# Attention, token mix, feed-forward and DFT kernel: VectorE in source order in the first group, fewer weight steps there, an earlier second batch, other homes for temporaries

## The chip, the cores and the metric

The kernel runs on one core of a Trainium2 chip. The metric is the device time of one execution in microseconds (us); three executions of the kernel before took 1892.73 to 1894.17 us, with a median of 1893.1 us.

## The reference

The computation, cut to what matters (8 batches, 8 heads, 576 tokens, head size 64, model size 512, feed-forward size 2048, all float32):

```
# attention with keys and values averaged over 8 tokens: 72 keys a head
k_p = k.reshape(B, H, 72, 8, D).mean(axis=3); v_p = the same of v
attn = softmax(q @ k_p.T / 8);  x = (attn @ v_p), heads side by side: B x 576 x 512
# token mix of rank 32, feed-forward 1
u = x + (x.T @ U @ V).T
x = u + relu(u @ moe_w1) @ moe_w2
# DFT mix over tokens and model size, layernorm, feed-forward 2
u = x + real(fft(fft(x, axis=tokens), axis=model))
un = (u - mean(u)) / sqrt(var(u) + 1e-6)
out = u + relu(un @ moe2_w1) @ moe2_w2
```

The four feed-forward weights arrive as float64. Each is turned into two float32 halves whose sum carries it; so is each activation (`hh` and `hl`, or `hw` for both in one tile), and one product becomes three matmuls.

## The kernel before, in words

Tokens go through the feed-forwards in blocks of 256. A first loop takes the first twelve blocks through feed-forward 1 (in groups: blocks 0 and 1 together, then one block each); later loops take the remaining six and all of feed-forward 2 in pieces of 512 tokens. The feed-forward size is cut into 16 tiles, f = 0 to 15. **Prologue.** `prep(0)` loads the pooled keys' and values' raw data of batch 0 (`kT`, `vr`) and reduces them over 8 tokens on VectorE (`kp`, `vp`); `first` runs the five attention tiles of batch 0 (scores on TensorE, maximum on VectorE, exponentials on ScalarE, the exponentials transposed and copied to `e` or a scratch tile `scr`, a product with `v`, and a division `x`, here a `scr` too). `mix_split` ends with `hst` (a copy on ScalarE, the remainder on VectorE), `mix_mm` multiplies it by `vst` and adds the result to the five x tiles, and `block_prep` transposes blocks 0 and 1 into `utx`, split in halves. **Groups.** Group 0 is "wide", with two blocks: 16 tiles f of `st1` (`h<-utx,w`), relu into `hh` and `hl` (or `hw` for odd f), and `st2` (`o<-w,hh` and so on) one tile behind.

Around `st1` and `st2` the loop steps lanes, which are Python generators: a (attention of later batches), mix, w (weights), prep (`prep` of the next batch: `kT` and `vr` through two buffers named `raw`, then the `kp` and `vp` reductions), p (`block_prep` of the next group) and d (the DFT). Of the w lane, `w_first` runs in the prologue and in group 0. For each f it loads two raw tiles (`wraw`, 512 KB each), makes a high half by bit operations (three ScalarE passes L144, L147, L108 and two VectorE passes L151, L152 for each tile of 128 x 512 words) and has GpSimd subtract (`w<-scr,w`), then the finished halves are written out (`wc`). `w_combine` follows (`wo`).

The order of instructions on an engine is chosen by a scheduler that simulates the program and moves instructions ahead of one another where it sees room; in a region under `tc.manual_schedule` the named engines keep source order. Before, ScalarE is named from group 1 on, and VectorE nowhere. All loads and stores go through SP's queue in SP's order, and a load into a reused buffer waits on SP until the buffer is free, with everything behind it.

Of the kernel before, what the change touches and what calls it, by code (L numbers as in the profile page):

```python
# [10 lines left out]
I32 = mybir.dt.int32  # L11
# [28 lines left out]
NOP = 12  # L40
NRING = 4
QAHEAD = 3
F64_BIAS = float.fromhex("0x1p-112")
# [3 lines left out]
def kernel(  # L47
# [30 lines left out]
    W = {}  # L78
    state = {"n": 0, "free": False, "m": "s1", "u": 0, "slot": 0, "x1": 0, "u2": 0, "op": 0, "clock": 0, "busy": False, "late": None, "tick": 0, "banks": ("s0", "s1", "hu")}

# [78 lines left out]
    def w_first(tmp):  # L159
        raws, ts = {}, {}  # L160

        def loads(upto):
            while len(raws) < min(NF, upto) and (len(raws) < (NF - 1 if state["free"] else 5) or NF - 2 in ts):
                f = len(raws)
                raws[f] = [wp.tile([128, 1024], I32, tag=f"w{k}_{f}", name="wraw") for k in range(2)]
                for k in range(2):
                    nc.sync.dma_start(out=raws[f][k], in_=(w1a, w2a)[k][f].bitcast(I32))
        def done(f):
            for k in range(2):
                w = wp.tile([128, 2, 512], F32R, tag=f"w{k}_{f}", name="w")  # L170
                W[k, f] = w
                split(w[:, 0], w[:, 1], ts[f][k].bitcast(F32), nc.gpsimd)
        loads(2)
        yield
        for f in range(NF + 1):
            loads(f + 3)
            while len(raws) < min(NF, f + 1):
                yield
                loads(f + 3)
            if f == NF - 1:  # L180
                done(f - 1)
            if f < NF:
                if f < NF - 2:
                    t = scratch(f % 2)
                    t = [t[:, 512 * k:512 * k + 512].bitcast(I32) for k in range(2)]
                else:
                    t = [tmp().bitcast(I32) for k in range(2)]
                ts[f] = t
                for k in range(2):
                    high(raws[f][k], 512, t[k], True)  # L190
            yield
            if f and f != NF - 1:
                done(f - 1)
            if f < NF:
                for k in range(2):
                    bits(raws[f][k], 512, t[k])
                yield
# [132 lines left out]
    class Attn:  # L330
        def __init__(self, c):
# [5 lines left out]
            self.ust = p1.tile([128, 5, 4, RANK], F32R, name="ust")  # L337
            self.usf = scratch(21)[:, 0:20 * RANK].rearrange("p (t g r) -> p t g r", t=5, g=4)
            self.vst = p1.tile([128, 640], F32R, name="vst")
# [5 lines left out]
            self.done = {}  # L345
            self.xq = [scratch(12 + t) for t in range(5)]
            self.x0 = [z[:, 0:512] for z in self.xq]
# [39 lines left out]
        def prep(self, b):  # L387
# [3 lines left out]
            self.kp[b] = (kp, vp)  # L391

            def load(i):
                t = scratch(2 + i) if b == 0 else self.tmp()
                if i < 4:
# [65 lines left out]
        def tile_steps(self, b, t, alt=0, before=None):  # L461
# [8 lines left out]
            for p in range(NPAIR):  # L470
                o = sc[p // 2][:n, (p % 2) * 144:(p % 2) * 144 + 144]
                mm(o, q[:, p, :n], self.k[:, p], p % 2 == 0, True)
            if 5 * b + t + QAHEAD >= 5:
                self.q_load(5 * b + t + QAHEAD)
            if before:
                before()
            sf = scratch(3 + alt) if alt else self.s
            if alt:
# [15 lines left out]
            nc.tensor.transpose(e1[:, :n], sf[:n, 512:640], ident[:n, :n])  # L494
            e = scratch(4 + 2 * alt, 640) if alt else p1.tile([128, 640], F32, tag="e", name="e")
            e = e.rearrange("p (c k) -> p c k", c=5)
# [519 lines left out]

    def rest(j):
        for t in range(NT):
            res[j, t] = mp.tile([128, DM], F32, tag="u", name="ur")
            r0 = j * T + t * 128  # L1020
            nc.sync.dma_start(out=res[j, t], in_=ud[r0:r0 + 128, :])
# [64 lines left out]
    def lane_prep(at):  # L1086
        for b in range(1, B):
            while b - 1 not in started or (b == 2 and state["slot"] < 11):
                yield
# [39 lines left out]
    for _ in g:  # L1129
        pass  # L1130
    lanes["w"] = w_first(at.cv)
    lanes["uv"] = at.setup_uv()
# [3 lines left out]
    for _ in f:  # L1136
        step("uv")
        step("w")
    with urgent():
        at.mix_split(0)  # L1140
    step("w")
    lanes["prep"] = lane_prep(at)
    for t in range(5):
        with urgent():
            at.mix_mm(0, t, at.x0[t])
        if t % 2:
            step("w")
        step("prep")
    state["u"] = S
    lanes["a"] = lane_a(at)  # L1150
    lanes["mix"] = lane_mix(at)
    for j in range(2):
        g = block_prep(j, at.x0[2 * j:])
        more = True
        while more:
            with urgent():
                more = not next(g, 1)
            if more:
                step("w")
    state["free"] = True  # L1160
    hq = []
    df = []
# [25 lines left out]
    slot = 0  # L1188
    order = ExitStack()
    for gi, js in enumerate(groups):  # L1190
        if gi == 1:
            order.enter_context(tc.manual_schedule(engines={mybir.EngineType.Activation}))
        wide = len(js) > 1
        last = js[-1] == 2 * SB - 1
        tags = (("o0", "o1"), ("h1", "m"))
        for f in range(NF):
# [30 lines left out]
            for i in range(2 if wide else 1):  # L1227
# [229 lines left out]
```

## Time and profile before

| what | value |
|---|---|
| median of three executions | 1893.1 us (1892.73 to 1894.17) |
| the profiled execution | 1888.01 us, its span 1886.2 us |
| TensorE busy | 1821.1 us (97%), weight loads 1634.8 us |
| VectorE busy | 1039.7 us (55%) |
| ScalarE busy | 715.7 us (38%) |
| GpSimd busy | 194.8 us (10%) |
| DMA | 394.41 MB, 209 GB/s in the mean |

The span is from the first to the last instruction of the profiled execution. PE is TensorE, PEld its weight loads, DVE is VectorE, ACT is ScalarE, POOL is GpSimd, SP the engine that issues the DMAs. A bracket behind a row of a timeline is the engine's idle time ahead of it and what ended it.

### The profile page before, as it was taken

The page shows a single profiled execution, that of the slowest core. Times are in us where ns is not written, and L with a number is a line of the kernel's source. Part 1 is how long each engine was busy: PE and PEld are TensorE (multiplying, and loading weights), DVE is VectorE, ACT ScalarE, POOL GpSimd, SP SyncE. Part 2 cuts the span into 40 slices and gives each one's busy share as a digit, 9 for nine tenths or more (in the row PEclk, how much of TensorE's full clock was granted, in tenths as well). Part 3 has the DMA queues.
Part 4 walks back from the last instruction along what each step waited for, and adds up shares of the span by engine and source line. Part 5 has one row for each costly group of instructions (what it writes and reads, how often), then busy time and mean ns, then how long its engine had stood idle before and what let it go on. Part 6 is the DMA issues. An engine that isn't in the chain of part 4 may idle for free.

```text
span 1886.2 us, 31833 instructions
## 1 busy us (share of the span) xinstructions
PE 1821.1 (97%) x11492; PEld 1634.8 (87%) x11492; DVE 1039.7 (55%) x2379; ACT 715.7 (38%) x2186; POOL 194.8 (10%) x341
## 2 busy tenths in 40 slices
PE   5789999999999999999999999999999999999999
PEld 3678888888989898899998889899999899989998
DVE  7774575656565544554456655555565444444332
ACT  7672444444434332433324332333333323232321
POOL 3440131222210000000010100000100000000000
PEclk9899999999999999999999999999999999999999
DMA  9754475758575524667677766666676674756563
GB/s 361 255 174 128 144 229 158 244 179 248 164 243 163 176 73 150 220 219 245 216 237 253 276 223 229 227 222 230 225 241 216 213 238 172 238 179 231 182 208 132
DMA packets 265789, 394.41 MB, mean 209 GB/s; under 512 B 61664, under 2 KB 92480, under 8 KB 265632
## 3 DMA queue, kind: packets, MB, share of 16 engines
q1 hardware_dynamic: 264704, 388.97, 62.3%
q0 software_dynamic: 928, 3.40, 0.5%
q8 instruction: 91, 1.49, 0.3%
q14 instruction: 66, 0.54, 0.1%
HBM read 312.73 MB, written 79.56 MB: 208 GB/s over the span
## 4 chain that ended last, share of the span: by engine, by line
PE 62%; DVE 2%; DMA 2%; issue 0%; ACT 0%; SPq 0%; DVEq 0%; ACTq 0%
PE h L112 27%; PE o L112 16%; PE m L112 7%; PE hu L112 7%; PE s L112 4%; PE s L889 1%; DMA w<-wd 0%; DMA R<-x1d 0%; DMA wr<-wc 0%; DMA out<-ur 0%; DMA ur<-u2d 0%; DMA wd<-cv 0%; DVE hl L1278 0%; DVE bs L865 0%; DVE ur L105 0%
## 5 line engine op out<-in xcount | busy, mean ns | idle before, releaser
L112 PEld LDWEIGHTS h<-x,wr 128*128 128x128 f32 x4032 | 527.6, 191 | 24.5 <-DVE side L105 0.8
L112 PE MATMUL h<-x,wr 128*128 128x256 f32 x4032 | 547.9, 284 | 0.2 <-DVE side L105 0.2
L112 PE MATMUL o<-w,hh 128*128 128x512 f32 x1440 | 417.4, 400 | 4.9 <-ACT hh L998 2.5
L112 PE MATMUL h<-utx,w 128*128 128x256 f32 (+1 forms) x2232 | 321.7, 289 | 9.2 <-DVE hl L999 3.8
L112 PEld LDWEIGHTS h<-utx,w 128*128 128x128 f32 x2232 | 301.2, 191 | 29.5 <-DVE hl L999 6.4
L112 PEld LDWEIGHTS o<-w,hh 128*128 128x128 f32 x1440 | 251.0, 190 | 43.5 <-ACT hh L998 5.6
L112 PE MATMUL o<-w,hl 128*128 128x512 f32 x720 | 239.1, 395 | 1.7 <-DVE hl L999 1.7
L105 DVE TENSOR_TENSOR side<-h,side 128x256 f32<-128x256 f32 x192 | 106.3, 554 | 137.8 <-PE h L112 136.9
L112 PEld LDWEIGHTS o<-w,hl 128*128 128x128 f32 x720 | 131.5, 189 | 25.4 <-DVE hl L999 2.1
L1272 ACT ACTIVATE hh<-side 128x256 fp32r<-128x256 f32 x192 | 100.0, 521 | 118.8 <-DVE side L105 112.5
L1272 ACT ACTIVATE hh<-h 128x256 fp32r<-128x256 f32 x96 | 36.8, 383 | 253.2 <-PE h L112 250.8
L1278 DVE SCALAR_TENSOR_TENSOR hl<-h,hh 128x256 fp32r<-128x256 f32 x96 | 40.7, 424 | 158.8 <-ACT hh L1272 158.8
L1278 DVE SCALAR_TENSOR_TENSOR hl<-side,hh 128x256 fp32r<-128x256 f32 x192 | 105.9, 551 | 28.2 <-ACT hh L1272 28.1
L489 ACT ACTIVATE s<-s,mx 128x72 f32<-128x72 f32 x296 | 90.6, 334 | 58.5 <-DVE mx L486 57.5
L112 PE MATMUL m<-w,hh 128*128 128x512 f32 x400 | 109.8, 395 | 0.0
L112 PE MATMUL hu<-w,hh 128*128 128x512 f32 x384 | 104.8, 394 | 0.0
L102 POOL TENSOR_TENSOR wo<-wo 128x256 fp32r<-128x256 f32 x88 | 69.1, 801 | 289.6 <-ACT wo L108 242.8
L998 ACT ACTIVATE hh<-h 128x256 fp32r<-128x256 f32 x158 | 61.4, 389 | 80.5 <-PE h L112 77.8
L999 DVE SCALAR_TENSOR_TENSOR hl<-h,hh 128x256 fp32r<-128x256 f32 x158 | 65.7, 417 | 32.7 <-ACT hh L998 32.1
L102 DVE TENSOR_TENSOR x<-ul,x 128x256 fp32r<-128x256 f32 x154 | 59.3, 421 | 42.2 <-ACT x L108 42.0
L112 PEld LDWEIGHTS m<-w,hh 128*128 128x128 f32 x400 | 69.1, 190 | 9.2
L1317 ACT ACTIVATE side<-h 128x256 f32<-128x256 f32 x96 | 36.7, 383 | 99.4 <-PE h L112 99.4
(252 smaller groups left out, 2390.3 us busy)
## 6 DMA issues: line engine op xcount, KB each, us to landing
wr<-wc SPq DMA_DIRECT2D x336, 512.0 KB
wc<-wo SPq DMA_DIRECT2D x88, 256.0 KB
x<-x SPq DMA_DIRECT2D x56, 256.0 KB
ur<-ud SPq DMA_DIRECT2D x36, 256.0 KB
x1d<-ur SPq DMA_DIRECT2D x36, 256.0 KB
ul<-u2d SPq DMA_DIRECT2D x36, 256.0 KB
ur<-u2d SPq DMA_DIRECT2D x36, 256.0 KB
out<-ur SPq DMA_DIRECT2D x36, 256.0 KB
```

The source lines that it names most:

```text
L102: eng.tensor_tensor(out=o, in0=a, in1=b, op=ALU.subtract)
L105: eng.tensor_tensor(out=o, in0=a, in1=b, op=ALU.add)
L112: nc.tensor.matmul(o, a, b, start=start, stop=stop, skip_group_check=True)
L489: nc.scalar.activation(out=s[:n, a], in_=v[:, k], func=ACTF.Exp, bias=mx[:n, a:a + 1], accum_out=sm[:n, a:a + 1])
L889: nc.tensor.transpose(o[:, k * 128:k * 128 + 128], u[:, k * 128:k * 128 + 128], ident)
L998: nc.scalar.activation(out=hh, in_=p, func=ACTF.Relu)
L999: nc.vector.scalar_tensor_tensor(out=hl, in0=p, scalar=0.0, in1=hh.bitcast(F32), op0=ALU.max, op1=ALU.subtract)
L1272: nc.scalar.activation(out=hh[:, i], in_=c, func=ACTF.Relu)
L1278: nc.vector.scalar_tensor_tensor(out=hl[:, i], in0=c, scalar=0.0, in1=hh[:, i].bitcast(F32), op0=ALU.max, op1=ALU.subtract)
L1317: nc.scalar.activation(out=sb, in_=v, func=ACTF.Copy)
```

## The change

- VectorE keeps source order in group 0 (beside ScalarE, which did so only from group 1 on). From group 1 on nothing changes in this.
- In group 0 the w lane is stepped once for each block of a tile f, where it was stepped twice for three tiles in four.
- `w_first` may have 12 tiles f of raw weights loaded in the late prologue and 15 after it (before: 5, then 15); for the first five f one of two high passes is on VectorE (`L147 TENSOR_SCALAR`) instead of ScalarE; half of its temporaries are `wo` tiles instead of scratch.
- The three q tiles of batch 1 are loaded after `mix_split`, where they were loaded in the first attention tiles.
- The prep lane is stepped twice with each tile of `mix_mm`, and batch 2 may begin at slot 9 instead of 11.
- The rows to which block 1's result is added (`ur<-ud`) are loaded at f = 12 into `cv` tiles, where they were loaded after block 0's end.

```
+    "most": 5 (in state)
-  while len(raws) < min(NF, upto) and (len(raws) < (NF - 1 if state["free"] else 5) or NF - 2 in ts):
+  while len(raws) < min(NF, upto) and (len(raws) < state["most"] or NSCR + 1 in ts):
...
+        def temps(f):
+            if f < NSCR and f % 4 < 2:
+                t = scratch(f % 2)
+                return [t[:, 512 * k:512 * k + 512].bitcast(I32) for k in range(2)]
+            return [tmp().bitcast(I32).rearrange("p h x -> p (h x)") for k in range(2)]
...
-                    high(raws[f][k], 512, t[k], True)
+                    high(raws[f][k], 512, ts[f][k], k or f >= 5)
...
-            if 5 * b + t + QAHEAD >= 5:
+            if b:
                 self.q_load(5 * b + t + QAHEAD)
...
-            while b - 1 not in started or (b == 2 and state["slot"] < 11):
+            while b - 1 not in started or (b == 2 and state["slot"] < 9):
...
-    lanes["w"] = w_first(at.cv)
+    lanes["w"] = w_first(at.wo)
...
+    state["most"] = NF - 4
     with urgent():
         at.mix_split(0)
     step("w")
+    for i in range(QAHEAD):
+        at.q_load(5 + i)
...
         step("prep")
+        step("prep")
...
+        if gi == 0:
+            order.enter_context(tc.manual_schedule(engines={mybir.EngineType.Activation}))
+            first_group.enter_context(tc.manual_schedule(engines={mybir.EngineType.DVE}))
         if gi == 1:
-            order.enter_context(tc.manual_schedule(engines={mybir.EngineType.Activation}))
+            first_group.close()
...
+            if wide and f == 12:
+                rest(js[1], at.cv)
...
-                for name in ("p", "mix", "w", "prep", "w") if f % 4 else ("p", "mix", "w", "prep"):
+                for name in ("p", "mix", "w", "prep", "w") if f % 4 and not wide else ("p", "mix", "w", "prep"):
...
-                    rest(prev[0][1])
```

How the change moves instructions is read at three places. A number after a name tells buffers apart.

**SP, the head of the program.** Before, SP issues the three q tiles of batch 1 first, then the four `kT` tiles of batch 0:

```order
L442 DMA q<-qT 128x4x128 x3
L396 DMA scr_139<-kT 128x576
L396 DMA scr_141<-kT 128x576
L396 DMA scr_143<-kT 128x576
L396 DMA scr_145<-kT 128x576
L442 DMA scr_132<-qT 128x4x128
```

Now the `kT` tiles come first:

```order
L395 DMA scr_139<-kT 128x576
L395 DMA scr_141<-kT 128x576
L395 DMA scr_143<-kT 128x576
L395 DMA scr_145<-kT 128x576
L441 DMA scr_132<-qT 128x4x128
```

The three q loads have moved behind the first ten `wraw` loads.

**VectorE, from `hst` to the `utx` of blocks 0 and 1.** Before, bit operations of the weights and `wo` operations stand between the adds of `mix_mm` (L105 into `scr_132` to `scr_136`) and the `utx`:

```order
L102 TENSOR_TENSOR hst<-hu,hst 32x512
L152 SCALAR_TENSOR_TENSOR scr_510<-wraw,scr_510 128x512 x2
L151 SCALAR_TENSOR_TENSOR cv<-wraw,cv 128x512
L105 TENSOR_TENSOR scr_132<-o_496,scr_132 128x512
L105 TENSOR_TENSOR scr_133<-h_506,scr_133 128x512
L105 TENSOR_TENSOR wo<-w 128x256
L105 TENSOR_TENSOR scr_134<-s_515,scr_134 128x512
L151 SCALAR_TENSOR_TENSOR cv<-wraw,cv 128x512
L105 TENSOR_TENSOR scr_135<-o_522,scr_135 128x512
L152 SCALAR_TENSOR_TENSOR cv<-wraw,cv 128x512
L105 TENSOR_TENSOR scr_136<-h_539,scr_136 64x512
L102 TENSOR_TENSOR utx<-s_547,utx 128x4x128
```

Now none stands between them:

```order
L103 TENSOR_TENSOR hst<-hu,hst 32x512
L106 TENSOR_TENSOR scr_132<-o_498,scr_132 128x512
L106 TENSOR_TENSOR scr_133<-h_508,scr_133 128x512
L106 TENSOR_TENSOR scr_134<-s_531,scr_134 128x512
L106 TENSOR_TENSOR scr_135<-o_541,scr_135 128x512
L106 TENSOR_TENSOR scr_136<-h_561,scr_136 64x512
L103 TENSOR_TENSOR utx<-s_570,utx 128x4x128
L103 TENSOR_TENSOR utx<-o_586,utx 128x4x128
L103 TENSOR_TENSOR utx<-h_604,utx 128x4x128
L103 TENSOR_TENSOR utx<-s_621,utx 128x4x128
```

From the start to `hst`, VectorE has 18 weight operations of 128 x 512 (L151, L152) and 9 `wo` operations before, 27 (L147, L152, L153) and none now. On ScalarE, ahead of `hst`, 24 weight operations stand before and 28 now; ahead of the last copies of exponentials (`scr_445` before, `scr_439` now), 16 before and 23 now.

**VectorE and SP, the `vp` reductions of batch 1 in tiles f = 0 to 2 of group 0.** On VectorE before, they are spread between the relu operations of two to three tiles (`hw<-h_642` is f = 1, `hl<-h_733` f = 2, `hw<-h_818` f = 3):

```order
L414 TENSOR_REDUCE vp<-raw 128x64 x2
L999 SCALAR_TENSOR_TENSOR hw<-h_642,hw 128x256
L486 TENSOR_REDUCE mx<-s_1067 128x4
L999 SCALAR_TENSOR_TENSOR hl<-h_733,hh 128x256 x2
L151 SCALAR_TENSOR_TENSOR scr_776<-wraw,scr_776 128x512
L152 SCALAR_TENSOR_TENSOR scr_776<-wraw,scr_776 128x512
L151 SCALAR_TENSOR_TENSOR scr_776<-wraw,scr_776 128x512
L152 SCALAR_TENSOR_TENSOR scr_776<-wraw,scr_776 128x512
L999 SCALAR_TENSOR_TENSOR hw<-h_818,hw 128x256
L414 TENSOR_REDUCE vp<-raw 128x64
L151 SCALAR_TENSOR_TENSOR scr_715<-wraw,scr_715 128x512
L414 TENSOR_REDUCE vp<-raw 128x64
```

Now all five stand in a row, ahead of four weight operations and of `hw<-h_698`, which is f = 1:

```order
L410 TENSOR_REDUCE kp<-raw 128x72
L998 SCALAR_TENSOR_TENSOR hl<-h_642,hh 128x256
L410 TENSOR_REDUCE kp<-raw 128x72
L413 TENSOR_REDUCE vp<-raw 128x64 x4
L413 TENSOR_REDUCE vp<-raw 64x64
L152 SCALAR_TENSOR_TENSOR wo<-wraw,wo 128x512
L153 SCALAR_TENSOR_TENSOR wo<-wraw,wo 128x512
L152 SCALAR_TENSOR_TENSOR wo<-wraw,wo 128x512
L153 SCALAR_TENSOR_TENSOR wo<-wraw,wo 128x512
L998 SCALAR_TENSOR_TENSOR hw<-h_698,hw 128x256 x2
```

On SP before, the third and fourth `vr` loads come behind five `wraw` loads, and the fifth behind a `wc`:

```order
L442 DMA q<-qT 128x4x128
L205 DMA wc_120<-w 256x1x256
L167 DMA wraw<-w1a 128x1024
L167 DMA wraw<-w2a 128x1024
L205 DMA wc_120<-w 256x1x256
L167 DMA wraw<-w1a 128x1024
L167 DMA wraw<-w2a 128x1024
L167 DMA wraw<-w1a 128x1024
L399 DMA raw<-vr 128x512 x2
L205 DMA wc_120<-w 256x1x256
L399 DMA raw<-vr 64x512
```

Now the third is behind five `wraw` loads, two `cv` loads and a `wc`:

```order
L398 DMA raw<-vr 128x512 x2
L205 DMA wc_120<-w 256x1x256
L168 DMA wraw<-w1a 128x1024
L168 DMA wraw<-w2a 128x1024
L168 DMA wraw<-w1a 128x1024
L1020 DMA cv<-ud 128x512
L168 DMA wraw<-w2a 128x1024
L168 DMA wraw<-w1a 128x1024
L1020 DMA cv<-ud 128x512
L398 DMA raw<-vr 128x512
L205 DMA wc_120<-w 256x1x256
L398 DMA raw<-vr 128x512
```

Since `raw` has two buffers, the first `vr` load waits for the third `kp` reduction, the third `vr` for the first `vp`, and the fifth for the third `vp`.

## Rows read from the trace of the kernel before

**Rows 1.** The page, part 1: the span and the busy time of each engine.
```profile
span 1886.2 us, 31833 instructions
...
PE 1821.1 (97%) x11492; PEld 1634.8 (87%) x11492; DVE 1039.7 (55%) x2379; ACT 715.7 (38%) x2186; POOL 194.8 (10%) x341
```

**Rows 2.** Busy time by engine in 20 us stretches from the start.
```profile
0.00:20.00 20.00, 5.77 (x30) 5.53 (x31) 10.49 (x24) 7.64 (x33) 7.00 (x23) 1.00 0.96 299
20.00:40.00 20.00, 15.24 (x84) 11.10 (x84) 18.59 (x41) 20.00 (x83) 4.59 (x5) 1.00 1.03 407
40.00:60.00 20.00, 10.33 (x35) 6.53 (x33) 19.91 (x28) 15.65 (x30) 10.88 (x7) 0.66 1.04 404
```

**Rows 3.** What TensorE waited for before 62.1 us, in us, times, longest.
```profile
PE s L112 <- ACT k L421: 13.8, 1, 13.8
```

**Rows 4.** Timeline 0 to 15 us of SP, ACT, DVE: start, us, operation, [idle before].
```profile
0.74 1.56 SPq L442 DMA_DIRECT2D q<-qT  x3
...
8.90 1.28 ACT L147 ACT_TABLE_LOAD   x1 [8.90 <-DMA scr<-U]
...
12.86 0.89 ACT L421 ACTIVATE k<-kp 64x288 f32<-64x288 f32 x2 [0.67 <-DVE kp L411]
...
12.08 0.74 DVE L411 TENSOR_REDUCE kp<-scr 128x72 f32<-128x576 f32 x1
```

**Rows 5.** Timeline 40 to 64 us of ACT, DVE, POOL and PE.
```profile
46.88 0.60 ACT L550 ACTIVATE hst<-hu 128x512 fp32r<-128x512 f32 x1
...
49.27 0.69 DVE L102 TENSOR_TENSOR hst<-hu,hst 32x512 fp32r<-32x512 f32 x1
...
52.66 1.75 DVE L151 SCALAR_TENSOR_TENSOR cv<-wraw,cv 128x512 int32<-128x512 int32 x1
54.45 0.69 DVE L105 TENSOR_TENSOR scr<-o,scr 128x512 f32<-128x512 f32 x1
...
56.59 0.68 DVE L151 SCALAR_TENSOR_TENSOR cv<-wraw,cv 128x512 int32<-128x512 int32 x1
...
49.22 6.32 POOL L102 TENSOR_TENSOR w<-scr,w 128x512 fp32r<-128x512 f32 x4 [3.87 <-DMA wc<-w]
...
50.02 0.80 PE L112 MATMUL o<-hst,vst 128*128 128x512 f32 x1 [3.18 <-DVE hst L102]
...
57.93 0.99 PE L812 MATMUL s<-ident,scr 128*128 128x128 f32 x4
62.11 2.29 PE L112 MATMUL h<-utx,w 128*128 128x256 f32 x9 [3.19 <-DVE utx L102]
```

**Rows 6.** Timeline 60 to 100 us of SP, DVE, PE; DMA rate by 1 us.
```profile
70.33 0.60 SPq L167 DMA_DIRECT2D wraw<-w1a  x1
...
73.23 0.54 SPq L167 DMA_DIRECT2D wraw<-w1a  x1
78.23 0.92 SPq L399 DMA_DIRECT2D raw<-vr  x2
...
77.52 1.27 DVE L414 TENSOR_REDUCE vp<-raw 128x64 f32<-128x512 f32 x2
...
76.44 1.65 PE L112 MATMUL o<-w,hw 128*128 128x512 f32 x6
...
GB/s 384 193 47 189 333 227 37 160 286 96 260 308 337 311 292 391 427 410 406 383 369 47 8 0 0 0 0 0 0 90 172 113 273 298 28 242 44 56 280 338
```

**Rows 7.** Busy time by engine in three stretches of group 0.
```profile
62.10:79.50 17.40, 15.54 (x90) 13.40 (x90) 13.88 (x23) 11.29 (x35) 7.87 (x8) 0.90 0.80 271
79.50:128.00 48.50, 42.18 (x260) 35.10 (x259) 39.41 (x62) 35.95 (x99) 21.24 (x17) 1.00 0.50 158
128.00:194.00 66.00, 62.94 (x390) 56.29 (x388) 28.96 (x58) 22.23 (x81) 6.37 (x9) 0.97 0.45 130
```

**Rows 8.** Timeline 180 to 220 us of SP and PE: the end of group 0.
```profile
198.40 2.00 SPq L1021 DMA_DIRECT2D ur<-ud  x2
...
202.19 1.70 PE L112 MATMUL h<-utx,w 128*128 128x256 f32 x12 [1.68 <-DVE ur L105]
```

More of the change, by code (lines that the diff above doesn't have):

```diff
@@ L41 @@
 NRING = 4
+NSCR = 10
 QAHEAD = 3
@@ L78 @@
     W = {}
-    state = {"n": 0, "free": False, "m": "s1", "u": 0, "slot": 0, "x1": 0, "u2": 0, "op": 0, "clock": 0, "busy": False, "late": None, "tick": 0, "banks": ("s0", "s1", "hu")}
+    state = {"n": 0, "free": False, "m": "s1", "u": 0, "slot": 0, "x1": 0, "u2": 0, "op": 0, "clock": 0, "most": 5, "busy": False, "late": None, "tick": 0, "banks": ("s0", "s1", "hu")}
     def scratch(i, w=1024, dt=F32):
@@ L179, in w_first @@
                 loads(f + 3)
-            if f == NF - 1:
-                done(f - 1)
             if f < NF:
[L183 to L188, printed above, removed]
+                ts[f] = temps(f)
                 for k in range(2):
-                    high(raws[f][k], 512, t[k], True)
+                    high(raws[f][k], 512, ts[f][k], k or f >= 5)
             yield
-            if f and f != NF - 1:
+            if f:
                 done(f - 1)
@@ L195, in w_first @@
                 for k in range(2):
-                    bits(raws[f][k], 512, t[k])
+                    bits(raws[f][k], 512, ts[f][k])
                 yield
@@ L337, in __init__ @@
             self.ust = p1.tile([128, 5, 4, RANK], F32R, name="ust")
-            self.usf = scratch(21)[:, 0:20 * RANK].rearrange("p (t g r) -> p t g r", t=5, g=4)
+            self.usf = scratch(16)[:, 0:20 * RANK].rearrange("p (t g r) -> p t g r", t=5, g=4)
             self.vst = p1.tile([128, 640], F32R, name="vst")
@@ L345, in __init__ @@
             self.done = {}
-            self.xq = [scratch(12 + t) for t in range(5)]
+            self.xq = [scratch(2 + t) for t in range(5)]
             self.x0 = [z[:, 0:512] for z in self.xq]
@@ L393, in load @@
             def load(i):
-                t = scratch(2 + i) if b == 0 else self.tmp()
+                t = scratch(7 + i) if b == 0 else self.tmp()
                 if i < 4:
@@ L476, in tile_steps @@
                 before()
-            sf = scratch(3 + alt) if alt else self.s
+            sf = scratch(6 + alt) if alt else self.s
             if alt:
@@ L494, in tile_steps @@
             nc.tensor.transpose(e1[:, :n], sf[:n, 512:640], ident[:n, :n])
-            e = scratch(4 + 2 * alt, 640) if alt else p1.tile([128, 640], F32, tag="e", name="e")
+            e = scratch(8 + alt, 640) if alt else p1.tile([128, 640], F32, tag="e", name="e")
             e = e.rearrange("p (c k) -> p c k", c=5)
@@ L1015, in st2, with rest @@
             mm(o, hl[:, c], w[:, 0], False, f == NF - 1)
-    def rest(j):
+    def rest(j, tile=lambda: mp.tile([128, DM], F32, tag="u", name="ur")):
         for t in range(NT):
-            res[j, t] = mp.tile([128, DM], F32, tag="u", name="ur")
+            res[j, t] = tile()
             r0 = j * T + t * 128
@@ L1160 @@
     state["free"] = True
+    state["most"] = NF - 1
     hq = []
@@ L1189 @@
     order = ExitStack()
+    first_group = ExitStack()
     for gi, js in enumerate(groups):
+        if gi == 0:
+            order.enter_context(tc.manual_schedule(engines={mybir.EngineType.Activation}))
+            first_group.enter_context(tc.manual_schedule(engines={mybir.EngineType.DVE}))
         if gi == 1:
-            order.enter_context(tc.manual_schedule(engines={mybir.EngineType.Activation}))
+            first_group.close()
         wide = len(js) > 1
```

## The prediction

> **What bounds the kernel now.** I read the page's busy times first: TensorE works for 1821.1 us of a span of 1886.2 [rows 1]. Some 65 us are idle, and a gain must come out of them or out of matmuls that run at the lower clock. The table of busy times by stretch shows where: in the first 20 us TensorE is busy for 5.77, in the next 20 for 15.24, in the third for 10.33, there at a granted clock of 0.66, so partly at the 1.2 GHz level [rows 2]; the prologue holds 28.7 us of the 65. Group 0 follows from 62.1 us: idle 1.86, 6.32 and 3.06 us in its three stretches (17.40 − 15.54 and so on), with a clock of 0.90 and 0.97 in the first and the last [rows 7]. What the change touches lies in these 200 us; the remaining 1,690 keep their code, their order rules and their bound, TensorE itself.
>
> Inside the prologue the bound changes hands. TensorE's first matmul waits 13.8 us for `k` [rows 3], which waits for the `kp` reductions, and these for `kT`, issued behind three q tiles [rows 4]. Then ScalarE has no idle time at all from 20 to 40 us [rows 2]. From `hst` on VectorE is the chain: ScalarE's half starts at 46.88, VectorE's only at 49.27, and st1 begins at 62.11, having waited for `utx` [rows 5].
>
> **The change part by part** (minus is a gain).
>
> *A, the start.* Three q tiles are 3 x 0.26 = 0.79 MB; at the 0.30 to 0.41 MB/us of the first stretches [rows 2] that is 1.9 to 2.6 us of transfer ahead of `kT`. The reductions also stand together now, and the table load, which waited until 8.90 for U [rows 4], waits for nothing. The last reduction began at 12.08 and `k` at 12.86 [rows 4]. The small operations that stood between the reductions go too, so I take −3.0, with −1.6 and −3.7 as ends.
>
> *B, ScalarE up to `hst`.* Seven more weight operations come ahead of the last copy of exponentials; a ScalarE pass of 128 x 512 takes 0.60 [rows 5], so +4.2 less A's 3.0 makes that copy 1.2 us late. Ahead of `hst` it is only four more, and VectorE has fewer things between, so I take `hst` at 47.5 instead of 46.88 (46 to 50).
>
> *C, `hst` to st1.* Before: 62.11 − 46.88 = 15.2 us, in which VectorE worked on weights too, one pass of them for 1.75 us [rows 5]. Now the chain is 0.60 on ScalarE, 0.69 on VectorE, 0.80 for the first product [rows 5], then five adds and three `utx` remainders that follow at about 0.6 (a 0.69 operation overlaps the next by a tenth): 4.9. With 0.2 for hand-overs that is 7.2; the transposes, 0.99 a tile [rows 5], run beside the adds. So st1 would begin at 54.7 and not 62.1: **−7.4 for A to C**, −10 and −5 as ends. The weight passes pushed back are hidden: eleven halves are ready at st1, and a tile f uses two.
>
> *D, the five `vp` reductions in a row.* This is the price. VectorE now can't pass them, and `hw` of f = 1 is behind. The first `vr` load can be issued only after the third `kp`, which stands behind the first `hl`: st1 from 54.7, `hl` near 60, load issued at 60.5, landed near 63. The third `vr` needs the first `vp`, and has on SP's queue five `wraw` (2.6 MB), two `cv` and one `wc` (0.8 MB) ahead. Do these delay it? Before, five `wraw` issued from 70.33 to 73.23 kept the DMA at 0.3 to 0.4 MB in each us until 81 [rows 6], and the `vr` loads issued at 78.23 fall into that. 3.4 MB at 0.4 are 8.4 us from 61: the third `vr` lands at 69.5 to 70. The fifth needs the third `vp`: a further trip (two loads issued from 198.40 had arrived when an add of 0.69 let TensorE go at 202.19, so at most 3.1 [rows 8]; I take 2.5) and lands near 73. One `vp` (0.64, two take 1.27 [rows 6]) and four weight passes of 0.68 [rows 5] make it 76.4 when `hw` starts, and 76.8 when it is there (0.4, an estimate: half the columns of such a pass). TensorE needs it 14.3 us after st1's begin (76.44 less 62.11) less its 1.9 of idleness [rows 5 to 7]: 67. So it stands for 9.7, where before it was idle for 1.9; matmuls after such a gap may run at the lower level for a while, as the 0.66 around the wait for `hst` shows [rows 2], which I put at 2. 9.7 − 1.9 + 2: **+10.** If the queue were empty, three trips in turn and the same passes would end near 71: +4. If the fifth load, too, waits behind others and GpSimd slows the passes: +14.
>
> The Trainium skill, in "DMA: Bandwidth & Descriptors", section "Two DMAs through the same engine are not ordered", says that the descriptors in one queue of one DMA engine start in order. The row agrees with it; without such an order a `vr` load could go past the `wraw`, and D would be near its +4.
>
> *E, the rest of group 0.* From 79.5 to 194 us TensorE idled 9.4 us, and 66 us at 0.97 cost 2 more [rows 7]: 11.4. Relu operations now can't be overtaken by weight passes that the scheduler pulled forward, and a tile f carries four VectorE passes, 2.7 us, of its own instead of bunches; VectorE is busy for 39.41 of 48.50 [rows 7], 6.6 of some 8 us a tile, so there is room. But attention in source order can itself make TensorE wait for exponentials: I leave 0.9 us for each of five attention tiles, 4.4. **−7**, ends −3 and −11.
>
> *F, the end of group 0.* Block 1's residual is in `cv` since f = 12, so the 1.68 us wait for `ur` [rows 8] goes: **−1.5**, ends 0 and −3.
>
> *G.* The fewer weight steps, the earlier second batch and the new homes of temporaries cost nothing by themselves: raw weights run four to six tiles ahead, which is the cover; if it were gone, each missing f would cost one load and seven passes, about 5 us. The kernel after group 0: 0, within 4 either way, since the DFT starts at most a tile later.
>
> Sum: −7.4 + 10 − 7 − 1.5 = −5.9. The profiled execution took 1888.0 (its span 1886.2), 5.1 below the median; the sum is a difference, so 1882 on its scale and **1887.2** on the median's. A measurement tells about 0.2% from no change, 3.8 us: below 1889.3 is faster, above 1896.9 slower.
>
> **The rivals.**
>
> *1. The `vp` chain is short*, because the `wraw` loads have landed by then or are issued later. For it: DMA engines were idle around 82 to 88 us [rows 6]. Against: the order of SP's queue. D is +4 or less: about 1881.
>
> *2. The prologue gets no shorter.* DMA is at 0.96 to 1.04 of its engines' time up to 60 us [rows 2], and ScalarE is full; if the weights' arrival or seven more passes set `hst`, at 50 and not 47.5, and the rest of C is lost to waits for transposes, then A to C is −2 and the total −2 + 10 − 7 − 1.5 = −0.5: about 1892.6.
>
> *3. In-order VectorE loses in group 0: slower.* While GpSimd ran from 49.22 for 6.32 us, a VectorE pass took 1.75, against 0.68 at 56.59 when it did not [rows 5]. The place is each tile f in which two subtractions of GpSimd meet four passes: if one such collision of 1.07 us a tile stands ahead of `hl`, and the cover of TensorE is used up, ten tiles cost 10.7 instead of E's −7: −5.9 + 7 + 10.7 = +11.8, about 1905. It turns the verdict once the collisions cost over 0.25 us a tile beyond E's loss (1.1 + 2.7 = 3.8). Against it: the same collisions occurred before, and the idle time of VectorE is 19% there.
>
> The Trainium skill, in "SBUF — State Buffer", section "SBUF: two separate sides", calls the port pair that VectorE and GpSimd share an exclusive lock: a VectorE operation with two SBUF inputs waits out a GpSimd operation that reads SBUF. The row agrees in kind, and by that rule every pass that meets a subtraction waits for the rest of it.
>
> **How the numbers follow.** The forecast (within 4 us of 1887) 0.45, rival 1 0.22, rival 2 0.20, rival 3 0.13. Rival 1 and four fifths of the forecast are faster: 0.58. A fifth of the forecast and most of rival 2 are the same: 0.28. Rival 3 and a remainder are slower: 0.14. The range 1877 to 1897 holds rivals 1 and 2 and leaves out most of rival 3 and a still better first group.
>
> **What would show it.** Right: the first matmul at 10 to 11; `hst` on ScalarE at 47 to 48 with VectorE's directly behind it; st1 at 54 to 55; one wait of TensorE of 8 to 11 us for `hw` within 62 to 78, VectorE idle in it for `vr` loads and DMA engines full; then under 6 us of waits until group 1. Wrong: st1 after 58 (B or C), a wait for `hw` under 4 us (D), waits for `hl` at every tile (E), or a change of over 4 us behind 220 us (G), which would come from the scheduler's other order of the later groups.

## The result, and the profile after

The changed kernel takes 1921.26 us (median of four, 1918.22 to 1925.39) against 1892.91 us: a ratio of 1.015, with a 95% interval of 1.013 to 1.017. It is slower by 28 us; the forecast was 1887.2 us. Its profiled execution took 1921.51 us, its span 1919.7, 33.5 more than the span before, which was profiled in a short execution.

The page, part 1 [rows 1], and the busy times by stretch [rows 2] of the changed kernel:

```profile
span 1919.7 us, 31854 instructions
...
PE 1834.7 (96%) x11496; PEld 1644.6 (86%) x11496; DVE 1043.7 (54%) x2383; ACT 714.2 (37%) x2180; POOL 193.3 (10%) x341
```

```profile
0.00:20.00 20.00, 7.57 (x35) 6.81 (x35) 11.51 (x28) 9.15 (x43) 7.46 (x25) 1.00 0.96 314
20.00:40.00 20.00, 15.10 (x74) 11.79 (x75) 19.68 (x37) 19.69 (x74) 5.68 (x5) 0.85 1.05 391
40.00:60.00 20.00, 12.62 (x40) 8.60 (x38) 16.76 (x24) 9.80 (x19) 10.27 (x7) 0.64 1.05 405
60.00:80.00 20.00, 11.05 (x72) 9.74 (x72) 8.06 (x14) 9.34 (x18) 4.66 (x5) 0.88 0.72 247
80.00:100.00 20.00, 10.94 (x61) 9.77 (x62) 10.31 (x19) 10.13 (x31) 4.22 (x5) 0.70 0.31 98
```

TensorE does almost the same matmuls (11,496 against 11,492). Of the 33.5 us, 19.9 are idle time and 13.6 are a longer busy time of these matmuls; from 60 to 100 us the granted clock is 0.88 and 0.70, where it was 0.91 and 1.00 before. A simple table finds the places: the start of st1 (the row `h<-utx,w` in TensorE's timeline) at seven points, in us of each profiled execution. The first loop ends with group 10.

| kernel | f = 0 | f = 2 | f = 10 | f = 15 | group 1 | group 8 | span |
|---|---|---|---|---|---|---|---|
| before | 62.1 | 79.5 | 147.8 | 181.2 | 194.0 | 615.7 | 1886.2 |
| changed | 60.4 | 91.8 | 172.0 | 203.2 | 216.6 | 646.6 | 1919.7 |
| change less before | −1.7 | +12.3 | +24.2 | +22.0 | +22.6 | +30.9 | +33.5 |

**The prologue.** TensorE's waits up to 62 us in the changed kernel, by what it waited for (us in total, times, longest), against 13.8, 3.2 and 3.2 for the first, third and fourth before [rows 3, 5]:

```profile
PE s L113 <- ACT k L420: 11.5, 1, 11.5
PE hu L113 <- DVE scr L508: 6.6, 3, 4.3
PE o L113 <- DVE hst L103: 1.4, 1, 1.4
...
PE h L113 <- DVE utx L103: 1.1, 1, 1.1
```

The first matmul is 2.3 us earlier. But the wait for `scr` L508, the division of an attention tile on VectorE, has grown from 2.4 us to 6.6, and `hst` is late. The same wait before:

```profile
PE hu L112 <- DVE scr L509: 2.4, 2, 2.0
```

The stretch from 37 to 62 us of the changed kernel, VectorE and TensorE:

```profile
39.95 2.39 DVE L153 SCALAR_TENSOR_TENSOR wo<-wraw,wo 128x512 int32<-128x512 int32 x2
...
42.26 1.40 DVE L410 TENSOR_REDUCE kp<-raw 128x72 f32<-128x576 f32 x2
...
44.51 0.68 DVE L508 TENSOR_TENSOR scr<-s,sm 128x512 f32<-128x512 f32 x1
...
46.21 3.44 DVE L152 SCALAR_TENSOR_TENSOR scr<-wraw,scr 128x512 int32<-128x512 int32 x2
...
50.17 0.68 DVE L508 TENSOR_TENSOR scr<-o,sm 128x512 f32<-128x512 f32 x1
...
53.64 0.69 DVE L103 TENSOR_TENSOR hst<-hu,hst 32x512 fp32r<-32x512 f32 x1 [2.20 <-ACT hst L549]
...
36.87 3.03 PE L113 MATMUL s<-v,e 128*128 128x128 f32 x10 [0.69 <-ACT e L496]
...
45.24 2.07 PE L113 MATMUL hu<-scr,scr 128*128 128x512 f32 x2 [4.27 <-DVE scr L508]
47.11 2.87 PE L113 MATMUL o<-v,scr 128*128 128x128 f32 x10
50.90 2.07 PE L113 MATMUL hu<-scr,scr 128*128 128x512 f32 x2 [0.92 <-DVE scr L508]
...
60.36 1.82 PE L113 MATMUL h<-utx,w 128*128 128x256 f32 x13 [1.14 <-DVE utx L103]
```

The large loss is at the fourth of the five divisions. Its product was done at 39.90 (the profile models the ends of matmuls), but VectorE came to it at 44.51, behind weight passes, one of them stretched to 1.79 us beside a subtraction of GpSimd, and two `kp` reductions; TensorE waited 4.27 us for it. The last division (50.17) also has passes of 1.7 us ahead of it, but its product was done only at 49.98, so they cost it almost nothing. So `hst` is on VectorE at 53.64 and not at 49.27 [rows 5]; from there to st1 it is 6.7 us instead of 12.8, as the order said.

**The five `vp`.** SP's loads, VectorE and TensorE from 62 to 92 us:

```profile
65.89 1.32 SPq L398 DMA_DIRECT2D raw<-vr  x2
67.33 0.53 SPq L205 DMA_DIRECT2D wc<-w  x1
...
73.88 0.42 SPq L398 DMA_DIRECT2D raw<-vr  x1
...
82.48 0.54 SPq L398 DMA_DIRECT2D raw<-vr  x1
...
65.12 0.75 DVE L410 TENSOR_REDUCE kp<-raw 128x72 f32<-128x576 f32 x1
...
81.76 0.69 DVE L413 TENSOR_REDUCE vp<-raw 128x64 f32<-128x512 f32 x1 [10.71 <-DMA raw<-vr]
...
85.20 0.68 DVE L413 TENSOR_REDUCE vp<-raw 64x64 f32<-64x512 f32 x1 [1.37 <-DMA raw<-vr]
...
88.59 0.41 DVE L998 SCALAR_TENSOR_TENSOR hw<-h,hw 128x256 fp32r<-128x256 f32 x1
...
66.40 3.04 PE L113 MATMUL h<-utx,w 128*128 128x256 f32 x24
...
89.06 1.22 PE L113 MATMUL o<-w,hw 128*128 128x512 f32 x2 [17.17 <-DVE hw L998]
```

The third `kp` (65.12) frees the first `vr` load, which SP issues at 65.89 with all other loads behind it. The `wc`, five `wraw` and two `cv` follow from 67.33; the third `vr` is issued at 73.88 and arrives at 81.76, the fifth is issued at 82.48 and arrives at 85.20. Only then come the four weight passes and, at 88.59, `hw` of f = 1, for which TensorE has waited 17.17 us. Before, TensorE went on with `hw` at 76.44 [rows 6].

**Tiles 2 to 11.** One of three tiles that look alike (at 102, 133 and 164 us):

```profile
131.28 0.69 DVE L508 TENSOR_TENSOR x<-s,sm 128x512 f32<-128x512 f32 x1 [2.80 <-PE s L113]
...
133.28 1.80 DVE L152 SCALAR_TENSOR_TENSOR wo<-wraw,wo 128x512 int32<-128x512 int32 x1
135.11 1.68 DVE L153 SCALAR_TENSOR_TENSOR wo<-wraw,wo 128x512 int32<-128x512 int32 x1
...
138.04 0.42 DVE L998 SCALAR_TENSOR_TENSOR hl<-h,hh 128x256 fp32r<-128x256 f32 x1
...
133.24 3.01 POOL L103 TENSOR_TENSOR w<-wo,w 128x512 fp32r<-128x512 f32 x2 [5.01 <-ACT w L109]
...
138.51 0.73 PE L113 MATMUL o<-w,hl 128*128 128x512 f32 x2 [2.34 <-DVE hl L998]
...
140.10 4.45 PE L113 MATMUL h<-utx,w 128*128 128x256 f32 x24
```

VectorE waits 2.80 us for an attention product, with four weight passes and both `hl` behind that wait; then GpSimd's subtraction starts with the passes and the first two take 1.80 and 1.68. TensorE waits 2.34 for `hl`, and the st1 behind it takes 4.45, where that of f = 1, at 66.40, took 3.04.

**The start of group 1.** VectorE and TensorE there:

```profile
219.81 0.75 DVE L410 TENSOR_REDUCE kp<-raw 128x72 f32<-128x576 f32 x1 [2.56 <-DMA raw<-kT]
...
221.22 4.65 PE L113 MATMUL h<-utx,w 128*128 128x256 f32 x22 [3.42 <-DVE utx L103]
```

The wait for `ur` is gone [rows 8], but TensorE waits 3.42 for `utx`, and the operation on `utx` (at 220.49) stands behind a `kp` that waited 2.56 for its load.

### The profile page after: what moved, and what is told of

Same layout as the page of the kernel before. It is cut to its first block, busy times and chain, and to the rows that moved or that the text cites. A ratio compares the mean times of both kernels' runs of the same rounds, so it can differ in the third digit from the quotient of the medians.

```text
span 1919.7 us, 31854 instructions
## 1 busy us (share of the span) xinstructions
PE 1834.7 (96%) x11496; PEld 1644.6 (86%) x11496; DVE 1043.7 (54%) x2383; ACT 714.2 (37%) x2180; POOL 193.3 (10%) x341
## 4 chain that ended last, share of the span: by engine, by line
PE 67%; DMA 2%; DVE 2%; ACT 1%; SPq 0%; issue 0%; DVEq 0%; ACTq 0%
PE h L113 29%; PE o L113 18%; PE m L113 7%; PE hu L113 7%; PE s L113 4%; PE s L888 1%; DMA ud<-x 1%; DMA wc<-wo 0%; DMA raw<-kT 0%; DMA x<-x 0%; PE s L492 0%; DMA wd<-cv 0%; DVE hl L1287 0%; DVE w L103 0%; ACT hh L1281 0%
## 5 line engine op out<-in xcount | busy, mean ns | idle before, releaser
L113 PE MATMUL h<-utx,w 128*128 128x256 f32 (+1 forms) x2236 | 327.7, 293 | 7.1 <-DVE utx L103 4.6
L113 PEld LDWEIGHTS h<-utx,w 128*128 128x128 f32 x2236 | 307.0, 195 | 26.7 <-DVE utx L103 5.1
L113 PEld LDWEIGHTS m<-w,hh 128*128 128x128 f32 x400 | 69.1, 190 | 9.3
L113 PEld LDWEIGHTS hu<-w,hh 128*128 128x128 f32 x384 | 66.0, 190 | 8.6
```

The costliest lines, as they stand in the source:

```text
L113: nc.tensor.matmul(o, a, b, start=start, stop=stop, skip_group_check=True)
```

## The experiments

Each was compared with the kernel before on its own chip, so between chips the ratios tell more than the medians. All but one compute the whole reference.

**Is it VectorE's order, or something else in the change?** The line that puts VectorE in source order is taken out of the changed kernel:

```
-            first_group.enter_context(tc.manual_schedule(engines={mybir.EngineType.DVE}))
```

> The change without VectorE's source order in group 0; all else as changed. Theory A (VectorE's order makes both losses of group 0: the five vp reductions in a row, +18.7 us, and the late hl and hw in tiles 2 to 11, +10.8): TensorE's wait of 17.2 us for hw falls under 4 us, st1 of tile 11 starts within 3 us of the kernel before, and the time is 1888 to 1897 us. Theory B (the later raw weight loads, the fewer weight steps or the new homes of temporaries make the loss, whatever VectorE's order): at least 1910 us.

Measured: 1889.96 us (1888.69 to 1892.52), ratio 0.9986 (0.9977 to 0.9995). TensorE's longest wait from its first to its third st1 (59.6 to 72.4 us):

```profile
PE h L113 <- DVE utx L103: 0.6, 1, 0.6
```

The time falls into theory A's range: in the changed kernel the whole loss hangs on this line. Its st1 starts are 59.6, 72.4, 147.9, 178.3, 193.1, 615.8, span 1887.8; against them the changed kernel, same but for the order, loses 0.8 in the prologue, 18.6 from f = 0 to 2, 4.7 up to f = 10, nothing up to group 1 (+0.8, −1.4), 7.3 up to group 8 and 1.1 later: 31.9 in all. The 0.8 is no difference: nine of the kernels here, these two among them, run the same operations in the same order on every engine up to st1, and st1 starts at 57.6 to 61.3 us in them. The opposite edit, the kernel before with only both engines' order:

```
...
+        if gi == 0:
+            order.enter_context(tc.manual_schedule(engines={mybir.EngineType.Activation}))
+            first_group.enter_context(tc.manual_schedule(engines={mybir.EngineType.DVE}))
         if gi == 1:
-            order.enter_context(tc.manual_schedule(engines={mybir.EngineType.Activation}))
+            first_group.close()
```

> The kernel before with VectorE and ScalarE in source order in group 0 and nothing else. Here the vp reductions stand one by one. Theory A: the order alone costs what tiles 2 to 11 lost, less what the prologue gains because no weight pass stands between hst and utx: 1893 to 1903 us, with waits for hl and hw at several tiles. Theory B: 1885 to 1894 us, since the homes, the loads and the steps are those of before.

Measured: 1919.79 us, ratio 1.0145 (1.0127 to 1.0163), 17 us over theory A's upper end, so its size is a miss; and since both engines change here, the run does not tell which of the two orders is the cause (ScalarE's alone follows below). Starts: 57.2, 69.1, 156.9, 190.9, 215.6. Here st1 begins 4.9 us earlier and there is no long wait for `vp`, yet tiles 2 to 10 take 87.8 us (68.3 before) and the way from tile 15 to group 1 takes 24.7 (12.8).

**Are the five `vp` in a row the price?** One of the two prep steps a mix tile is taken out, which spreads them:

```
         step("prep")
-        step("prep")
```

> The change with the prep lane stepped once with each mix tile, as before, so that the vp reductions stand one by one between the hl and hw. Theory A: the wait of 17.2 us for hw becomes one of at most 4, the collisions of tiles 2 to 11 stay, and the time is 1902 to 1909 us. Theory B: 1917 to 1925 us.

Measured: 1919.98 us, ratio 1.0142 (1.0118 to 1.0165). The time is in theory B's range and theory A's number is a miss: the 17.2 us wait is gone (f = 2 at 72.0), and up to tile 15 (183.1) the kernel is 20 us ahead of the changed one, but group 1 begins at 214.6. Busy times in the stretch ahead of group 1:

```profile
195.00:200.00 5.00, 2.70 (x11) 1.29 (x9) 3.66 (x8) 2.76 (x17) 0.00 (x0) 0.85 0.88 265
200.00:205.00 5.00, 4.53 (x17) 4.11 (x16) 2.10 (x4) 1.60 (x4) 0.00 (x0) 0.50 0.64 149
205.00:210.00 5.00, 2.73 (x11) 1.47 (x10) 3.51 (x8) 2.85 (x17) 0.00 (x0) 0.84 0.69 209
```

Batch 1 was prepared later, its last attention tiles stand at the end of group 0 with no st1 beside them, at a clock of 0.50 to 0.85, and the saved time is spent there. So the loads have to be early and the `vp` not waited for. In the next kernel batch 1's `vr` tiles have buffers of their own:

```
-                t = scratch(7 + i) if b == 0 else self.tmp()
+                t = scratch(7 + i) if b == 0 or (b == 1 and i > 3) else self.tmp()
...
-            for i in range(ahead):
+            for i in list(range(ahead)) + (list(range(4, 9)) if b == 1 else []):
...
-                if i + ahead < 9:
+                if i + ahead < (4 if b == 1 else 9):
```

> The change with the five vr tiles of batch 1 in scratch tiles of their own, loaded with the first kT tiles of that batch, so that no vp reduction waits for a load; batch 1 begins as early as in the change. Theory C (the wait of 17.2 us for hw is the price of the loads, and stepping the prep lane once only moved its price to the end of group 0, because batch 1 then came late): the wait falls under 2 us, st1 of group 1 follows st1 of tile 15 by some 13 us as in the change and not by 31, and the time is 1902 to 1910 us. Theory D (whatever is saved early comes back at the end of group 0): 1916 us or more.

Measured: 1908.25 us, ratio 1.0073 (1.0058 to 1.0088); f = 0 to 2 takes 14.2 us instead of 31.4, tile 15 to group 1 13.4. Theory C holds: −17.2 there, +5.4 in the prologue, where st1 comes at 65.8 since the `vr` loads and reductions now lie there; by the medians 13 us less in all.

**What do tiles 2 to 11 pay for?** Four edits of the changed kernel. The subtraction on VectorE from f = 6 on:

```
-                split(w[:, 0], w[:, 1], ts[f][k].bitcast(F32), nc.gpsimd)
+                split(w[:, 0], w[:, 1], ts[f][k].bitcast(F32), nc.gpsimd if f < 6 else nc.vector)
```

> The change with the subtraction that ends a weight half on VectorE instead of GpSimd from f = 6 on (two more VectorE passes of about 0.69 us a tile, no GpSimd beside them). Theory A1 (GpSimd's subtractions stretch the passes ahead of hl and hw in every third tile, 1.7 to 1.8 us instead of 0.69): the waits of 2.2, 2.3 and 3.8 us with the 4.5 us st1 behind them go, 8 to 11 us less, 1910 to 1914 us. Theory A2 (source order itself is the cause, whatever a pass takes): same or slower, 1919 to 1930 us.

Measured: 1936.9 us, ratio 1.0221 (1.0204 to 1.0237): the time is beyond both ranges, and theory A1 fails as tested. Tiles 2 to 10 take 96.0 us instead of 80.2; since the edit also puts two more passes a tile on VectorE, it does not tell what the collisions cost by themselves. The weight step ahead of the attention step:

```
+                if wide:
+                    step("w")
                 if wide or slot % 4:
                     step("a")
...
-                for name in ("p", "mix", "w", "prep", "w") if f % 4 and not wide else ("p", "mix", "w", "prep"):
+                for name in ("p", "mix", "prep") if wide else ("p", "mix", "w", "prep", "w") if f % 4 else ("p", "mix", "w", "prep"):
```

> The change with the weight step of group 0 ahead of the attention step in each block of a tile, so that the four weight passes no longer stand behind a VectorE instruction that waits for an attention product. Theory E1 (in tiles 2 to 11 VectorE stands idle for attention with the weight passes, hl and hw behind it): tiles 2 to 11 lose 3 to 8 us less, 1913 to 1918 us. Theory E2 (too much VectorE work a tile, wherever it stands): within 2 us of the change, or slower since attention comes later: 1919 us or more.

Measured: 1919.14 us, ratio 1.0129 (1.0114 to 1.0144); tiles 2 to 10 take 79.8. Theory E1's gain did not come: TensorE no longer waits for `hl` or `hw` in these tiles, but it waits 6.1 us for the exponentials `s` instead of 0.9, with attention now behind the weight passes. GpSimd's subtraction left out:

```
+                if f < 6:
                     split(w[:, 0], w[:, 1], ts[f][k].bitcast(F32), nc.gpsimd)
+                else:
+                    nc.scalar.activation(out=w[:, 0], in_=ts[f][k].bitcast(F32), func=ACTF.Copy)
+                    nc.gpsimd.memset(w[:, 1].bitcast(F32), 0.0)
```

> The change with GpSimd's subtraction left out from f = 6 on: the low half of those weights is set to zero by a GpSimd operation that reads no SBUF, so the output lacks those products' low halves; VectorE's passes and all else stay. Theory G (rival 3: GpSimd's subtractions stretch VectorE's passes ahead of hl and hw in every third tile): passes take 0.7 us everywhere in tiles 2 to 11, the waits of 2.2, 2.3 and 3.8 us and the st1 of 4.5 us behind them go, 1909 to 1914 us. Theory H (the passes' place and count matter, not the collisions): 1918 to 1923 us.

Measured: 1912.49 us, ratio 1.0109 (1.0089 to 1.0129), in theory G's range; tiles 2 to 10 take 75.4, and no pass there takes over 1 us. So 4.8 of the 8.8 us by the medians lie in these tiles; 2.1 lie ahead of the first st1, where the edit changes nothing. TensorE's waits from 92 us on in the changed kernel (to 172) and in this one (to 175):

```profile
PE o L113 <- DVE hw L998: 6.0, 2, 3.8
PE o L113 <- DVE hl L998: 2.3, 1, 2.3
```

```profile
PE s L113 <- ACT e L500: 2.6, 2, 1.3
PE o L113 <- DVE hw L1002: 2.3, 1, 2.3
...
PE o L113 <- DVE hl L1002: 0.2, 1, 0.2
```

The subtraction one step earlier, with all work done:

```
+            if f > 5:
+                done(f - 1)
             yield
-            if f:
+            if 0 < f < 6:
                 done(f - 1)
```

> The change with the finished half of a weight tile copied and subtracted one step earlier from f = 6 on (with the high passes of the next f, not with its VectorE passes), all work done. If the collisions of GpSimd's subtraction with VectorE's passes are the loss of tiles 2 to 11, and not something else that leaving the subtraction out took away: 1910 to 1915 us, no pass over 1 us in tiles 5 to 11. If leaving work out was the gain: 1918 to 1923 us.

Measured: 1918.53 us, ratio 1.0157 (1.0143 to 1.0171), in the range of "leaving work out was the gain", and no gain by the ratio (1.015 without the edit); tiles 2 to 10 take 79.1, and of the passes from f = 5 on three still take over 1 us. The waits in this kernel, 92 to 175 us:

```profile
PE s L113 <- ACT e L498: 4.7, 2, 2.3
PE o L113 <- DVE hw L1000: 4.6, 3, 2.9
```

Both early buffers and early subtraction:

> The run with own vr tiles and the run before together. If the vp loads (13 us) and the collisions (9 us) are separate losses, they add up: 1897 to 1902 us, against 1890 us without VectorE's order. If one hides behind the other: 1904 us or more.

Measured: 1904.25 us, ratio 1.0082 (1.0069 to 1.0096), at the lower end of "one hides behind the other": beside the own buffers the earlier subtraction brings 4 us by the medians and nothing by the ratios. And without VectorE's order:

> The change with VectorE free in group 0 and the earlier subtraction. The scheduler can already move hl and hw ahead of a stretched pass, so little is left to gain: 1887 to 1891 us. If collisions cost there too, as in source order: 1881 to 1886 us.

Measured: 1897.4 us, ratio 1.0045 (1.0031 to 1.0058): over both ranges and no gain, against 0.9986 without this edit.

**Is it ScalarE's order?** In the kernel before, ScalarE alone is put in source order in group 0:

```
-        if gi == 1:
+        if gi == 0:
             order.enter_context(tc.manual_schedule(engines={mybir.EngineType.Activation}))
```

> The kernel before with ScalarE alone in source order in group 0 (VectorE free). Theory A (VectorE's order is the loss; ScalarE's keeps weight passes out of the stretch from hst to utx, since VectorE's passes need ScalarE's): st1 starts at 57 to 59 us instead of 62.1, group 0 keeps its length, 1886 to 1890 us. Theory F (ScalarE's order costs as much, as the waits for hh and s in the run with the order alone suggest): 1896 us or more.

Measured: 1914.38 us, ratio 1.01 (1.0084 to 1.0117): theory F. ScalarE's order alone costs 20 of the 27 us that both orders cost in the kernel before, and the starts of st1 are nearly the same in both. St1 comes at 58.3, tiles 2 to 10 take 87.4. One row of ScalarE, and TensorE's largest wait from 69 to 160 us, in this kernel:

```profile
75.34 0.66 ACT L144 ACTIVATE scr<-wraw 128x512 int32<-128x512 uint32 x1 [3.03 <-POOL w L102]
```

```profile
PE o L112 <- ACT hh L998: 12.9, 3, 5.5
```

With the old homes a weight pass into one of two scratch tiles waits 3.03 for GpSimd, and `hh` (at 78.90) stands behind it. The change has new homes and a single weight step; the steps are tried without the new homes (the order alone, one weight step for each block and two prep steps):

> The kernel before with VectorE and ScalarE in source order in group 0, one weight step for each block there, and the prep lane stepped twice; the loads, homes and residual as before. Theory I (these two parts of the change repair what source order costs: tiles 2 to 9 lost 21 us with the old step counts and 7 in the change, the end of group 0 13.5 and 3.5): those two losses go, and a wait for the vp loads comes in at f = 1, so 1905 to 1916 us with st1 of group 1 some 13 us behind tile 15. Theory J (they repair nothing): 1918 us or more without a shorter end of group 0.

Measured: 1924.95 us, ratio 1.0172 (1.0151 to 1.0193). The mechanisms of theory I are there (tiles 2 to 10 take 79.2 instead of 87.8, tile 15 to group 1 10.9 instead of 24.7), and so is a wait of 15.3 us for `hw`; its sum is a miss: from group 1 to group 8 this kernel takes 440 us, with the order alone 429. From 65 to 172 us ScalarE's weight passes wait 1.0 us for GpSimd, where with ScalarE's order alone they waited 8.7. So in tiles 2 to 10 the steps do it with the old homes; that the new homes matter there isn't shown.

**The start and the prologue.** The q loads behind `mix_split`, on top of ScalarE's order, and the reverse, q loads back at the head of the change without VectorE's order:

> As the run before, with the three q loads of batch 1 behind mix_split. If step A of the prediction is right in the start, the first matmul comes at 10 to 11.5 us instead of 13.8 and st1 another 1 to 3 us earlier: 1884 to 1888 us. If DMA or VectorE sets the rest of the prologue, st1 stays and the time is that of the run before within 2 us.

> The change with VectorE free in group 0 and the three q loads of batch 1 back at the head. If step A of the prediction is worth its 3 us at the end of the prologue: 1892 to 1894 us, st1 2 to 3 us later. If another engine sets the prologue's end: within 2 us of the run without VectorE's order, 1888 to 1892 us.

Measured: 1920.09 us, ratio 1.0131 (1.011 to 1.0152), st1 at 59.0 (58.3 without the move); and 1897.16 us, ratio 1.0024 (1.0013 to 1.0036), first matmul at 14.3 and st1 at 67.1 (11.3 and 59.6). All four ranges are missed. The move costs 6 us in the one and saves 7 in the other, by the ratios; the first matmul is 2 and 3 us earlier with it, but what is behind it decides. Batch 2 from slot 11:

> The change with VectorE free in group 0 and batch 2 from slot 11, as before. If the earlier second batch is what costs some 5 us between 377 and 616 us in all kernels with ScalarE's new order: 1884 to 1888 us. If not: 1888 to 1892 us.

Measured: 1898.5 us, ratio 1.0024 (1.0011 to 1.0037), over both ranges: by the ratios the earlier second batch is a gain of 7 us, and not what groups 2 to 8 lose (from group 1 to group 8 this kernel takes 439.9 us, with batch 2 from slot 9 422.7). The high passes back on ScalarE, VectorE free:

> The change with VectorE free in group 0 and all high passes on ScalarE, as before, so that five passes of 0.3 to 1.5 us leave VectorE in the prologue. Theory K (VectorE, busy for 38.4 of 41 us from 13 to 54 us, sets hst in the change, not ScalarE as step B took it): TensorE's waits for the scr that VectorE divides shrink from 8.7 us, st1 comes 1 to 3 us before the 59.6 of the run with VectorE free, 1886 to 1889 us. Theory L (ScalarE sets hst): st1 comes later by five passes of 0.6, 61 to 63 us, 1891 to 1894 us.

Measured: 1895.88 us, ratio 1.0 (0.999 to 1.0009). St1 comes at 61.4 instead of 59.6, as theory L said, but that is hardly beyond the spread of st1 above, and not for its reason. VectorE and TensorE in this kernel:

```profile
44.97 3.46 DVE L153 SCALAR_TENSOR_TENSOR scr<-wraw,scr 128x512 int32<-128x512 int32 x2
48.35 1.76 DVE L152 SCALAR_TENSOR_TENSOR scr<-wraw,scr 128x512 int32<-128x512 int32 x1
50.04 0.68 DVE L508 TENSOR_TENSOR scr<-o,sm 128x512 f32<-128x512 f32 x1
...
44.93 3.04 PE L113 MATMUL o<-v,scr 128*128 128x128 f32 x10 [1.05 <-ACT scr L496]
50.77 2.08 PE L113 MATMUL hu<-scr,scr 128*128 128x512 f32 x2 [2.80 <-DVE scr L508]
```

The waits for `scr` fall from 8.7 us to 3.4, as theory K said: the fourth division comes at 41.07 and not at 44.20. But now the last division, whose product was done at 47.97, stands behind three passes of 1.7 us beside GpSimd until 50.04, where the change had it at 50.17. What was saved at the fourth division is lost at the last.

## Why the prediction was wrong, point by point

Predicted sum −5.9; the profiled spans differ by +33.5.

- **A, B, C (−7.4; measured −1.7, and −0.8 to −4.5 in the nine kernels with this order up to st1).** A came out at −2.3. B is wrong: `hst` comes at 53.0 on ScalarE, not at 47.5, and VectorE sets it. I counted VectorE's 27 weight passes against 18 and priced none of them. With two `kp` reductions they hold up the fourth division by 4.6 us; with five passes fewer they hold up the last one. VectorE's order has no part in this: without it the order up to st1 is the same. C's chain took 6.7 us where 6.6 was said (from `hst` on VectorE). Rival 2 had the size of A to C (−2), but its reason was the weights' arrival or ScalarE; that it fits is luck.
- **D (+10; measured +14.0 from f = 0 to 2).** The mechanism is right in each link, and the first `vr` went out 5.5 us behind st1, as said (5.8). One term was mis-sized: the loads in front of the third `vr` took 14.4 us from their first issue (67.33 to 81.76), not 8.4. In that time the DMA moved 4.9 MB at 0.34 MB/us, where I counted 3.4 MB at 0.4; the two `vr` loads ahead of these, the third `vr` itself and loads issued behind it are in the 4.9. The fifth load took 2.7 (2.5 said). TensorE stood 17.2 us, not 9.7. Own buffers show that these loads are the cause. That +14 was also my upper end is luck: its reasons, a late fifth load and slow passes, did not occur.
- **E (−7; measured +9.7 from f = 2 to 15).** This is the step that failed, sign and all. I took the idle time before as a fault of the scheduler's order that source order would mend, and priced the waits that source order itself makes at 0.9 us for each attention tile. The runs show three waits of 2.2 to 3.8 us in its place, behind a row of attention product, weight passes and relu on VectorE. VectorE's order taken out of the change gives back 31 us over the whole kernel. In the kernel before, both orders cost 27 us, but ScalarE's alone 20, so that pair does not price VectorE's. Of the +9.7, 5.5 go with VectorE's order (105.9 us without it, 111.4 with it); the other 4.2 (101.7 before) are left without it, too, and most of them, 3.5, are a longer busy time of the same number of matmuls, at a granted clock of 0.97 instead of 1.00.
- **F (−1.5; measured +0.6 to group 1 and a new wait of 3.42).** The wait for `ur` went, one for `utx` took its place. Both lie behind the start of group 1, so the 3.42 is part of the +10.9 below.
- **G (0; measured +10.9 behind the start of group 1).** From group 1 to group 8 the kernel before takes 421.7 us, the changed one 430.0, without VectorE's order 422.7. Of the 8.3 us more in the changed one, 4.4 are idle time and 3.9 a longer busy time, at a granted clock of 0.98 instead of 1.00. But the kernel before with ScalarE's order alone takes 428.0, so VectorE's order isn't the only thing that does this; which one of the later moves it is stays open.

Rival 3 had the side right and the mechanism in part: the collisions are there, at three tiles, 1.6 to 1.8 us a pass. Of the signs of being wrong that the prediction named, st1 after 58 us and over 4 us behind 220 us came; waits for `hl` or `hw` came at three tiles, not at every one. Leaving the subtraction out gave back 4.8 us in tiles 2 to 10; moving it, with most passes unstretched, gave 1.1 there and nothing by the ratio, and other waits came in their place (`e`, 4.7). How much of the 5.5 us of VectorE's order in E is collision, and how much the wait for attention with `hl` behind it, isn't settled.

The Trainium skill, in "SBUF — State Buffer", section "SBUF: two separate sides", calls the port pair an exclusive lock for the whole instruction. The rows agree in kind: a pass of 0.68 takes 1.7 beside subtractions of 1.3 to 1.7 us, in the prologue as in group 0. But a pass that began before the subtraction did not wait for it, so rival 3 went too far with "every pass that meets a subtraction". I used the row in rival 3 alone and left it out of B, where one such pass (1.79 us) stood ahead of the fourth division.

## What to carry to other kernels

An engine in source order passes a wait on to all that stands behind it: before an engine is put in source order, list each instruction that waits for a load or for another engine's late product, and what stands behind it; five reductions with two buffers made a load chain for which TensorE waited 17 us. Idle time under a scheduler's order was no gain to be had by fixing the order here; the order alone, tried on the old kernel and for one engine at a time, is the cheapest test. A saving in front is worth something only if the work that it displaced isn't left bare at the end: look for the next barrier behind it.

## What the runs showed of the hardware

A VectorE pass with two SBUF inputs that takes 0.68 us alone took 1.2 to 1.8 when it began during a subtraction of GpSimd's: so in all twelve such places of the changed kernel up to 200 us. The six passes that began before the subtraction that they met kept 0.64 to 0.68. Behind a wait of 2.34 us TensorE's 24 matmuls of st1 took 4.45 us, at a granted clock of 0.64, against 3.04 at 1.00 at f = 1: there the stall cost 1.4 us more than its own length. Behind the wait of 17.17 us the clock was 0.50, the lower of its two levels, for 2.73 us, and st1 after that took 3.17.
